# Replacing sixteen TensorE matmuls by accumulating DMAs, and holding weight loads for them, in a gated attention and token-mixing kernel

## The chip, the cores and the metric

The kernel runs on one core of a Trainium2 chip. The metric is the device time of one execution in microseconds (us). The kernel before takes 165.4 us. On one core there are no other cores to compare with, so a run counts as "slow" only when it is over 1.5% above the fastest run of the same kernel; ratios use the fast runs alone.

Engine names in the profile: PE is the matmul engine (TensorE), PEld its weight loads, DVE is VectorE, ACT is ScalarE, POOL is GpSimd, SP is SyncE. POOL and SP mainly issue DMAs here. The granted clock is the share of TensorE's full speed that the profile shows as allowed, 1.00 being all of it.

## The reference, cut to what matters

```python
def reference(A_x, A_wqkv, A_wo, B_x, B_w1, B_b1, B_w2, B_b2, gate_w):   # S=2048, D=512, 32 heads of 16, F=1792
    g = sigmoid((x * gate_w).sum(-1, keepdims=True))                     # x = A_x
    # a: attention over 8 keys, at positions s, s-2, ..., s-14
    qkv = x @ wqkv
    logits = einsum("bhsd,bhswd->bhsw", q, k[gathered]) * 16 ** -0.5     # masked where s-2w < 0
    a = einsum("bhsw,bhswd->bhsd", softmax(logits), v[gathered]) @ wo
    # b: an MLP over the token axis
    u = gelu(einsum("bsd,sf->bdf", layernorm(x), w1) + b1)
    b = transpose(einsum("bdf,fs->bds", u, w2) + b2)
    return g * a + (1 - g) * b
```

## The kernel before

All instructions are handed to a small list scheduler in the kernel, with an estimated duration each. It fixes the order on each engine before the launch; at run time every engine takes its own list in order and waits on semaphores.

The attention logits are products on VectorE: for each of four groups `dl` of four head dimensions, q times shifted k, added into one buffer of 128 partitions by 8 shifts by tokens. Head `i` sits in partitions 4i to 4i+3, so a logit is the sum over four neighbouring partitions. The kernel does the 2048 tokens in two halves, `h` = 0 and 1, each in two parts `s_`. **Before**, TensorE forms that sum for each half with a 0/1 matrix `RP`, and ACT moves the result from PSUM to SBUF:

```python
def f_sum(h, b0, with_gate):                 # 16 matmuls of 512 columns, four at a time in column tiles
    ...                                      # (for h == 0 also the gate's 16 matmuls)
    for wp in range(4):
        for c in range(4):
            ins = e.matmul(ps[32 * c:32 * c + 32, 4 + wp, :], lhsT=RP, rhs=sub(PB[b0], ...), start=True, stop=True, tile_position=(0, 32 * c))
...
A("pe", f_sum(h, b0, h == 0), ..., name="sum%d" % h, prio=-100)
A("act", act(LOG[h], ps[:, 4:8, :], AF.Copy), 1.9, ..., name="lev%d" % h)
A("dve", tt(M4, LOG[h][:, 0:4, :], LOG[h][:, 4:8, :], ALU.max), ..., name="mx4_%d" % h)     # softmax follows
...
# the softmax weights are then spread from 32 to 128 partitions by four DMAs of 512 KB
prev = sch.dma("pool", ..., 524288, name="av%d_%d" % (h, c))
```

The weights multiply the values in eight units `u` of 256 tokens: a product (`avm`, 8192 elements per partition, 4.4 us), then three halving additions `ava`, `avb`, `avc`. For three units the first addition is an accumulating DMA of 1 MB, SBUF to SBUF, on POOL's queue:

```python
AVD = (3, 4, 5)
if u in AVD:
    sch.dma("pool", (lambda o_, i_: lambda e: e.dma_start(o_, i_, accum_op=ALU.add, ...))(pw(0, 4), pw(4, 4)), ..., name="avd%d" % u)
```

The MLP's weights stream in on SP's queue, W1 in seven loads of 1 MB, W2 in eight of 896 KB, each as soon as its buffer is free. The output stores are on the same SP queue:

```python
def ld_w2(j):
    w1ld[7 + j] = load("w2_%d" % j, W2S[j], w2v[:, :, 256 * j:256 * j + 256], F * 256 * 2, ["w2_%d" % j] + W2ALIAS[j], order=False,
                       after=[w1ld[6 + j]])           # 512-byte rows
def finish_tile(i):
    PE(f_wo(i, bank, 0, D), 0.87, ["ot%d" % (i // 2), "wo"], ...)                 # attention's output projection into the same PSUM bank
    A("act", act(OUTS[:, i % 4, :], ps[:, bank, :], AF.Identity, scale=..., bias=...), ...)   # four output buffers
    sch.dma("sp", ... e.dma_start(outv[:, i_, :], OUTS[:, i_ % 4, :]) ..., name="d_out%d" % i)
```

Of the kernel before, what the change touches and what calls it, by code (L numbers as in the profile page):

```python
# [12 lines left out]
S = 2048  # L13
# [56 lines left out]
class _Sched:  # L70
# [73 lines left out]
    def _pass(self, ops, extra, dma_bw, dma_lat):  # L144
# [21 lines left out]
        dma_free = 0.0  # L166
# [8 lines left out]
        while nleft:  # L175
            best = None
            for e in self.ENGS:
                lst = ready[e]
                if not lst:
                    continue  # L180
                bo = None
                bk = None
                for op in lst:
                    st = max(clock[e], rtime[op.idx])
                    if op.table is not None and loaded is not None and op.table != loaded:
                        st += 1.3
                    k = (st, -bl[op.idx] + 3.0 * op.prio, op.idx)
                    if bk is None or k < bk:
                        bk = k
                        bo = op  # L190
                if best is None or bk < best[0]:
                    best = (bk, bo)
            assert best is not None, "scheduler deadlock (cyclic deps?)"
            st = best[0][0]
# [6 lines left out]
            if op.is_dma:  # L201
                clock[e] = st + op.dur
                xs = max(st + 0.3, dma_free)
                xd = max(op.nbytes / dma_bw, 0.05)
                dma_free = xs + xd
                op.end = max(dma_free, clock[e]) + dma_lat
            else:
                op.end = st + op.dur
                clock[e] = op.end
# [98 lines left out]
def bass_gated_mix__sliding_local_dilated__mixer_token_mlp__prompt_kernel(nc, A_x, A_wqkv, A_wo, B_x, B_w1, B_b1, B_w2, B_b2, gate_w, out, dbg=None):  # L308
    with contextlib.ExitStack() as es:
# [11 lines left out]
        for b in range(3):  # L321
# [42 lines left out]
        W1H = [view(n_, BF16, [(256, NST), (1, 256)], extra=k_ * W1N)  # L364
               for n_, k_ in (("W1", 0), ("W1", 1), ("W1", 2), ("XT", 0), ("XT", 1), ("W1", 0), ("W1", 1))]
        W1R = ["w1s0", "w1s1", "w1s2", "w1x0", "w1x1", "w1s0", "w1s1"]

        def w2view(name, extra=0):
            return view(name, BF16, [(256, NFT), (1, 256)], extra=extra)
# [166 lines left out]
        def ld_w1(j):  # L536
            w1ld[j] = load("w1_%d" % j, W1H[j], w1v[:, :, 256 * j:256 * j + 256], S * 256 * 2, [W1R[j]] + (XTALL if j in (3, 4) else []), order=j < 3,
                           after=[w1ld[j - 1]] if j > 3 else [])

        def ld_w2(j):  # L540
            w1ld[7 + j] = load("w2_%d" % j, W2S[j], w2v[:, :, 256 * j:256 * j + 256], F * 256 * 2, ["w2_%d" % j] + W2ALIAS[j], order=False,
                               after=[w1ld[6 + j]])
# [39 lines left out]
        def f_q0(hb, dt):  # L582
            c0, c1 = ((0, 256), (256, 512), (0, 512))[hb]

            def fn(e):
                ins = None
                for dl in range(4):
# [26 lines left out]
        pe_q0(2, 3)  # L614
# [46 lines left out]
        kb0 = [bank_() for dl in range(2)]  # L661
        for k_ in range(2):
            for dl in range(2):
                PE(f_proj(1, dl, 0, kb0[dl], 2 * k_, 2 * k_ + 2), 0.44, XT0 + ["wk%d" % k_], ["b%d" % kb0[dl]], "pjk%d_0_%d" % (dl, k_))
                if k_ == 1:
                    evac(1, dl, 0, kb0[dl])
        for dl in range(2, 4):
# [37 lines left out]
        for t in range(NST):  # L705
            A("dve", (lambda t_: lambda e: e.tensor_scalar(out=X[:, t_, :], in0=X[:, t_, :], scalar1=col(RSTD, t_), scalar2=col(NMR, t_),  # L706
                                                           op0=ALU.mult, op1=ALU.add))(t), 0.33,
              reads=["rstd", "nmr", "st%d" % t], writes=["x%d" % t], name="ln%d" % t, prio=-10)


        def f_sum(h, b0, with_gate):
            def fn(e):
                ins = None
                if with_gate:
                    for dt in range(4):
                        for c in range(4):
                            ins = e.matmul(ps[32 * c:32 * c + 32, 3, :], lhsT=GWREP[:, dt, :],  # L717
                                           rhs=sub(XT, dt * S + c * UT_, [(HS, 2), (1, UT_)]),
                                           start=(dt == 0), stop=(dt == 3), tile_position=(0, 32 * c))
                for wp in range(4):  # L720
                    for c in range(4):
                        ins = e.matmul(ps[32 * c:32 * c + 32, 4 + wp, :], lhsT=RP, rhs=sub(PB[b0], (c // 2) * 4096 + 2 * wp * 512 + (c % 2) * UT_, [(512, 2), (1, UT_)]),  # L722
# [4 lines left out]
        LGB = ["b4", "b5", "b6", "b7"]  # L727
        PLAN = {0: (0, 1, 2), 1: (1, 2, 0)}
        PS = [["p%d_%d" % (b_, s_) for s_ in range(2)] for b_ in range(3)]
        qkd = {}  # L730
        for h in range(2):
            bb = PLAN[h]

            def qk(dl, b_, s_, h=h):
                sb = 2 * h + s_
                A("dve", tt(sub(PB[b_], s_ * 4096, [(512, NW), (1, 512)]), sub(QH[h], dl * HS + s_ * 512, [(0, NW), (1, 512)]),
                            sub(KH[h], dl * KR + PAD + s_ * 512, [(-2, NW), (1, 512)]), ALU.mult), 2.25,
                  reads=["q%d_%d" % (dl, sb), "k%d_%d" % (dl, sb)] + (["k%d_%d" % (dl, sb - 1)] if s_ else ["khalo" if h else "kpad"]),
                  writes=[PS[b_][s_]], name="qk%d_%d_%d" % (h, dl, s_))

            def qadd(x_, y_, s_, h=h):
                A("dve", tt(sub(PB[x_], s_ * 4096, [(1, 4096)]), sub(PB[x_], s_ * 4096, [(1, 4096)]), sub(PB[y_], s_ * 4096, [(1, 4096)]), ALU.add), 2.25,
                  reads=[PS[y_][s_]], writes=[PS[x_][s_]], name="qa%d_%d%d_%d" % (h, x_, y_, s_))
# [12 lines left out]
            for s_ in range(2):  # L756
                qk(3, bb[1], s_)
                qadd(bb[2], bb[1], s_)
            for s_ in range(2):
                qadd(bb[0], bb[2], s_)  # L760
            b0 = bb[0]
            A("pe", f_sum(h, b0, h == 0), 1.2 + (1.0 if h == 0 else 0), reads=PS[b0] + ["rp"] + ((XTALL + ["gwrep"]) if h == 0 else []),
              writes=LGB + (["b3"] if h == 0 else []), name="sum%d" % h, prio=-100, delay=0.2)
            if h == 0:
                A("act", act(E32, ps[:, 3, :], AF.Relu, scale=-1.0, bias=ZMAX), 0.6, reads=["b3"], writes=["e32"], name="zclip")
                A("act", act(EB, E32, AF.Exp, scale=-1.0, bias=ZMAX), 0.6, reads=["e32"], writes=["eb"], name="zexp", table=LOGEXP)
            A("act", act(LOG[h], ps[:, 4:8, :], AF.Copy), 1.9, reads=LGB, writes=["log%d" % h], name="lev%d" % h, prio=-30)
            if h == 0:
                A("dve", tt(psub(LOG[0], 0, 32, 0, [(UT_, NW), (1, PAD)]), psub(LOG[0], 0, 32, 0, [(UT_, NW), (1, PAD)]), MASK, ALU.add), 0.2,
                  reads=["mask"], writes=["log0"], name="msk", prio=-30)  # L770
            TR = ["s4", "s2", "s1"]
            A("dve", tt(M4, LOG[h][:, 0:4, :], LOG[h][:, 4:8, :], ALU.max), 0.65, reads=["log%d" % h], writes=["s4"], name="mx4_%d" % h, prio=-30)
            A("dve", tt(M2, M4[:, 0:2, :], M4[:, 2:4, :], ALU.max), 0.4, reads=["s4"], writes=["s2"], name="mx2_%d" % h, prio=-30)
            A("dve", tt(M1, M2[:, 0, :], M2[:, 1, :], ALU.max), 0.25, reads=["s2"], writes=["s1"], name="mx1_%d" % h, prio=-30)
            A("dve", tt(LOG[h], LOG[h], sub(M1, 0, [(0, NW), (1, UT_)]), ALU.subtract), 1.2, reads=["s1"], writes=["log%d" % h], name="msub%d" % h, prio=-30)
# [7 lines left out]
            A("dve", tt(ATT[h], ATT[h], sub(RB, 0, [(0, NW), (1, UT_)]), ALU.mult), 1.2, reads=["rb"], writes=["att%d" % h], name="nrm%d" % h, prio=-30)  # L783
# [3 lines left out]
            for c in range(4):  # L787
# [4 lines left out]
                al = []  # L792

# [15 lines left out]
        AVD = (3, 4, 5)  # L809
        AVB = (2, 0, 1)  # L810
        avlast = [None]

        def AV(fn, dur, **kw):
            avlast[0] = A("dve", fn, dur, after=[avlast[0]] if avlast[0] else [], **kw)

        def av_parts(u):
            b_ = AVB[u % 3]
# [17 lines left out]
        def av_add(u):  # L835
            res, pv, pw = av_parts(u)
            AV(tt(pw(0, 2), pw(0, 2), pw(2, 2), ALU.add), 1.19, writes=res, name="avb%d" % u)
            AV(tt(OT[:, u], pv[:, 0], pv[:, 1], ALU.add), 0.66, reads=res, writes=["ot%d" % u, OTRES[u]], name="avc%d" % u)

        todo = []  # L840
        for u in range(8):
            av_mult(u)
            if todo and todo[0] + 2 <= u:
                av_add(todo.pop(0))
            if u in AVD:
                todo.append(u)
            else:
                av_add4(u)
                if todo and u == 7:
                    av_add(todo.pop(0))  # L850
                av_add(u)


        def f_ph2(ft, bank, half):
            def fn(e):
                ins = None
                for st in range(8 * half, 8 * half + 8):
                    ins = e.matmul(ps[:, bank, :], lhsT=W1H[ft // 2][:, st, 128 * (ft % 2):128 * (ft % 2) + 128], rhs=X[:, st, :],  # L858
                                   start=(st == 0), stop=(st == NST - 1))
# [3 lines left out]
        MLPB = [1, 2, 0, 1, 2, 0, 3, 1, 2, 0, 3, 1, 2, 0]  # L863
        for ft in range(NFT):
            bank = MLPB[ft]
            for half in range(2):
                PE(f_ph2(ft, bank, half), 1.735, ["x%d" % t for t in range(8 * half, 8 * half + 8)] + [W1R[ft // 2]], ["b%d" % bank],
                   "ph2_%d_%d" % (ft, half))
            A("act", act(UT[:, ft, :], ps[:, bank, :], AF.Gelu_apprx_tanh, bias=col(B1C, ft)), 0.7,
              reads=["b%d" % bank, "b1c"], writes=["ut%d" % ft] + (["wq0", "wq1", "wq2", "wq3", "wk0", "wk1", "wv"] if ft == 0 else []), name="gel%d" % ft, table=GELU)  # L870
            if ft % 2 == 1 and ft // 2 + 5 <= 6:
                ld_w1(ft // 2 + 5)
# [4 lines left out]
        LAG = 5  # L877
        ring[0], ring[1] = 0, [3, 4, 5, 6, 7, 1, 2, 0]
        banks = {}

        def f_ph3(i, bank, half, c0=0, c1=D):
            def fn(e):
                ins = None
                for ft in range(7 * half, 7 * half + 7):
                    ins = e.matmul(ps[:, bank, 0:c1 - c0], lhsT=W2S[i // 2][:, ft, 128 * (i % 2):128 * (i % 2) + 128], rhs=UT[:, ft, c0:c1],  # L885
# [16 lines left out]
        def finish_tile(i):  # L902
            bank = banks[i]
# [5 lines left out]

        L = NST - 1  # L910
        for i in range(L):
            banks[i] = bank_()
        head = ((0, 0), (1, 0), (2, 0), (0, 1), (1, 1), (2, 1))
        for i, half in head + tuple((i, half) for i in range(3, L) for half in range(2)):
            bank = banks[i]
# [103 lines left out]
```

## Time and profile before

| | before |
|---|---|
| time, median (range) | 165.39 us (165.37 to 165.50, 3 runs) |
| span of the profiled run | 163.0 us |
| PE busy | 158.6 us, 97% |
| VectorE busy, and the end of its last unit | 151.1 us, 93%; 157.4 us |
| DMA engine time, loads and stores / POOL's queue | 51.6% / 27.3% of the 16 engines' span |

The summary page of the kernel before: busy time by engine; the DMA queues (q1 is SP's, q0 is POOL's: packets, MB, share of the 16 engines' span); the chain of waits by engine.

```profile
PE 158.6 (97%) x793; PEld 77.2 (47%) x808; DVE 151.1 (93%) x126; ACT 70.2 (43%) x100; POOL 12.0 (7%) x36
...
q1 hardware_dynamic: 41444, 22.06, 51.6%
q0 software_dynamic: 2512, 9.44, 27.3%
...
PE 97%; ACT 1%; issue 1%
```

PE is the bound. It has no gap of a microsecond after the start; the chain is PE almost from end to end.

### The profile page before, as it was taken

The numbers are of one execution on the slowest core, as the hardware profiler recorded it, in microseconds if no ns is written. First come the engines' busy times: TensorE is split into PE (matmuls) and PEld (weight loads), VectorE is DVE, ScalarE is ACT, GpSimd is POOL, SyncE is SP. The second block draws the span as 40 slices with busy tenths as digits, with TensorE's granted clock in tenths as the row PEclk, the third lists the DMA queues.
The fourth block names the chain that finished last, engine by engine and source line by source line (L and its number), as shares of the span: only waits on it lengthen the run. The fifth ranks groups of instructions, "written<-read, shape, count | busy, mean of one in ns | idle before, by whom it ended". The sixth has DMA issues, their size and how long they took to land.

```text
span 163.0 us, 1989 instructions
## 1 busy us (share of the span) xinstructions
PE 158.6 (97%) x793; PEld 77.2 (47%) x808; DVE 151.1 (93%) x126; ACT 70.2 (43%) x100; POOL 12.0 (7%) x36
## 2 busy tenths in 40 slices
PE   7999999999999999999999999999999999999993
PEld 4855555555544344444444344444444444444641
DVE  1789999999999999999999999999999999999961
ACT  3367677666771579662111348011111111111164
POOL 3000030020000000023000000003100222000000
PEclk9999999999999999999999999999999999999999
DMA  5999979729499095999998976981997899991014
GB/s 165 311 268 259 221 183 263 140 38 191 101 277 292 24 242 157 261 290 290 303 245 233 260 188 177 290 209 30 300 243 193 186 207 193 205 216 36 32 59 134
DMA packets 44685, 32.24 MB, mean 198 GB/s; under 512 B 7941, under 2 KB 42245, under 8 KB 44677
## 3 DMA queue, kind: packets, MB, share of 16 engines
q1 hardware_dynamic: 41444, 22.06, 51.6%
q0 software_dynamic: 2512, 9.44, 27.3%
q10 hardware_dynamic: 720, 0.62, 1.2%
q8 instruction: 6, 0.10, 0.2%
q14 instruction: 3, 0.02, 0.0%
HBM read 18.88 MB, written 2.10 MB: 129 GB/s over the span
## 4 chain that ended last, share of the span: by engine, by line
PE 97%; ACT 1%; issue 1%
PE ps L858 30%; PE ps L885 30%; PE ps L649 23%; PE ps L894 8%; PE ps L588 2%; PE ps L551 2%; PE ps L722 1%; ACT arena L453 1%; PE ps L717 1%; PE ps L567 1%; PE ps L604 0%
## 5 line engine op out<-in xcount | busy, mean ns | idle before, releaser
L450 DVE TENSOR_TENSOR arena<-arena 128x4096 bf16<-128x4096 bf16 (+8 forms) x79 | 131.9, 1718 | 1.6 <-ACT arena L453 0.6
L885 PE MATMUL ps<-arena 128*128 128x512 bf16 (+2 forms) x234 | 50.0, 366 | 0.2
L858 PE MATMUL ps<-arena 128*128 128x512 bf16 x218 | 48.5, 379 | 0.3
L453 ACT ACTIVATE arena<-ps,arena 128x512 bf16<-128x512 f32 (+1 forms) x30 | 21.8, 731 | 60.7 <-PE ps L894 37.7
L453 ACT ACTIVATE arena<-ps 128x512 bf16<-128x512 f32 (+3 forms) x53 | 32.9, 629 | 17.4 <-PE ps L649 10.9
L649 PE MATMUL ps<-arena 128*128 128x512 bf16 x173 | 38.0, 379 | 0.2
L885 PEld LDWEIGHTS ps<-arena 128*128 128x128 bf16 x238 | 22.8, 98 | 25.9
L858 PEld LDWEIGHTS ps<-arena 128*128 128x128 bf16 x224 | 21.7, 98 | 26.8 <-issue 0.8
L649 PEld LDWEIGHTS ps<-arena 128*128 128x128 bf16 x176 | 19.9, 113 | 18.0
L894 PE MATMUL ps<-arena 128*128 128x512 bf16 (+2 forms) x67 | 15.6, 366 | 0.1
L453 ACT ACTIVATE arena<-arena 128x16 f32<-128x16 f32 (+5 forms) x10 | 6.7, 678 | 9.7 <-DVE arena L450 9.6
L954 ACT ACT_TABLE_LOAD x7 | 9.0, 1283 | 2.8 <-issue 2.7
L894 PEld LDWEIGHTS ps<-arena 128*128 128x128 bf16 x68 | 6.5, 98 | 7.3
L692 DVE BATCH_NORM_STATS2 arena<-arena 128x6 f32<-128x512 bf16 x16 | 9.9, 679 | 0.1
L790 POOL DMA_DIRECT2D arena<-arena x8 | 4.3, 560 | 75.1 <-DVE arena L450 75.1
L706 DVE TENSOR_SCALAR arena<-arena 128x512 bf16<-128x512 bf16 x16 | 5.3, 404 | 0.0
L827 POOL DMA_DIRECT2D arena<-arena x3 | 3.6, 1209 | 17.7 <-DVE arena L450 17.7
L747 POOL DMA_DIRECT2D arena<-arena x2 | 2.5, 1268 | 30.6 <-DVE arena L692 20.2
L579 DVE CAST arena<-ps 128x256 bf16<-128x256 f32 x4 | 1.6, 422 | 3.2 <-PE ps L567 3.2
L588 PE MATMUL ps<-arena 128*128 128x256 bf16 (+1 forms) x27 | 3.8, 284 | 0.2 <-ACT arena L453 0.2
L551 PE MATMUL ps<-const-bfloat16-1.0 128*128 128x512 bf16 (+1 forms) x9 | 2.7, 483 | 0.8 <-PEq L1004 0.8
L588 PEld LDWEIGHTS ps<-arena 128*128 128x128 bf16 x28 | 2.9, 113 | 0.7 <-DVE arena L579 0.4
(30 smaller groups left out, 14.4 us busy)
## 6 DMA issues: line engine op xcount, KB each, us to landing
arena<-in_B_w_dram SPq DMA_DIRECT2D x7, 1024.0 KB, 6.8
arena<-in_B_w_dram SPq DMA_DIRECT2D x8, 896.0 KB, 9.4
arena<-arena POOLq DMA_DIRECT2D x5, 1024.0 KB, 9.7
arena<-arena POOLq DMA_DIRECT2D x8, 512.0 KB, 11.2
out_dram<-arena SPq DMA_DIRECT2D x15, 128.0 KB, 3.1
arena<-in_A_x_dram SPq DMA_DIRECT2D x3, 512.0 KB, 4.7
arena<-in_A_wqkv_dram SPq DMA_DIRECT2D x2, 256.0 KB, 3.8
arena<-in_A_wqkv_dram SPq DMA_DIRECT2D x1, 512.0 KB, 5.6
```

Source lines behind the costliest of these rows:

```text
L450: return lambda e: e.tensor_tensor(out=o_, in0=a_, in1=b_, op=op_)
L453: return lambda e: e.activation(out=o_, in_=i_, func=f_, **kw)
L551: ins = e.matmul(ps[:, 7, 0:n_], lhsT=C1, rhs=nc.const_aps.tensor(1.0, (128, n_), BF16), start=True, stop=True)
L588: ins = e.matmul(ps[:, dl, c0:c1], lhsT=sub(WQKV, dt * 3 * D + dl, [(4, 128)]), rhs=XT[:, dt, c0:c1], start=(dt == 0 and hb == 0), stop=(d ...
L649: ins = e.matmul(ps[:, bank, :], lhsT=sub(WQKV, dt * 3 * D + tn * D + dl, [(4, 128)]), rhs=XT[:, dt, sb * 512:(sb + 1) * 512], start=(dt = ...
L692: A("dve", (lambda t_: lambda e: e.bn_stats(out=ST6[:, t_, :], in_=X[:, t_, :]))(t), 0.67, reads=["x%d" % t], writes=["st%d" % t], name="s ...
L706: A("dve", (lambda t_: lambda e: e.tensor_scalar(out=X[:, t_, :], in0=X[:, t_, :], scalar1=col(RSTD, t_), scalar2=col(NMR, t_), op0=ALU.mu ...
L790: prev = sch.dma("pool", (lambda d_, s_: lambda e: e.dma_start(d_, s_))(dst, src), 524288, sch.dsem("av%d_%d" % (h, c)), issue=1.0, reads= ...
L858: ins = e.matmul(ps[:, bank, :], lhsT=W1H[ft // 2][:, st, 128 * (ft % 2):128 * (ft % 2) + 128], rhs=X[:, st, :], start=(st == 0), stop=(st ...
L885: ins = e.matmul(ps[:, bank, 0:c1 - c0], lhsT=W2S[i // 2][:, ft, 128 * (i % 2):128 * (i % 2) + 128], rhs=UT[:, ft, c0:c1], start=(ft == 0) ...
L894: ins = e.matmul(ps[:, bank, 0:c1 - c0], lhsT=OT[:, i // 2, dl, 128 * (i % 2):128 * (i % 2) + 128], rhs=WO[:, dl, c0:c1], start=False, sto ...
L954: e.preload_act_table_set(want)
```

## The change

The intent: take the second half's head sums off PE, the bounding engine (16 matmuls and one ACT eviction), and give them to DMAs that add in flight; keep the DMA engines clear for them by holding some W2 loads; and take work off VectorE. The parts:

1. Second half's head sums by 12 DMAs on POOL's queue: four add partition 4i+2 onto 4i and 4i+3 onto 4i+1 (256 KB each), four copy partition 4i into the logits (128 KB each), four add partition 4i+1 to them (128 KB each). I call them folds. The products are laid out anew for them.
2. W2 load 2 waits for the first-stage folds, W2 load 3 for the last fold, W2 load 6 for the last of the second half's weight broadcasts. I call these the holds.
3. The accumulating additions go to units 2, 4, 5; a new order of the units.
4. Block 0's last Q matmuls signal per `dl`, and K of block 0 is no longer started on the first half of its weights; the gate's matmuls move earlier; eight of sixteen normalizations move to ACT.
5. W1 and W2 loads have 1 KB rows; the two MLP matmuls are regrouped by four tiles and half contractions. The scheduler's own DMA model is changed too.

```diff
+            if h:
+                fas = {}
+                for s_ in range(2):
+                    for k_ in range(2):
+                        fas[s_] = fold("fa%d_%d%d" % (h, s_, k_), par(PB[b0], k_, [(4 * pst, 32), (1, 4096)], s_ * 4096), par(PB[b0], k_ + 2, ...),
+                             True, 550000, [PS[b0][s_]], ["fa%d_%d%d" % (h, s_, k_)])
+                for s_ in range(2):
+                    for k_ in range(2):
+                        for c in (2 * s_, 2 * s_ + 1):
+                            fl = fold("%s%d_%d" % ("fb" if k_ == 0 else "fc", h, c), psub(LOG[h], 32 * c, 32, 0, [(1, NW * UT_)]), par(PB[b0], k_, ...),
+                                 k_ == 1, 100000 * (1 + k_), [PS[b0][s_], "fa%d_%d%d" % (h, s_, k_)], ["log%d_%d" % (h, c)], ...)
+                folds += [fas[1], fl]
+            else:
+                A("pe", f_sum(b0), 1.0, ...)
+                A("act", act(LOG[h], ps[:, 4:8, :], AF.Copy), 1.9, ...)
...
         def ld_w2(j):
-            w1ld[7 + j] = load("w2_%d" % j, W2S[j], w2v[:, :, 256 * j:256 * j + 256], F * 256 * 2, ["w2_%d" % j] + W2ALIAS[j], order=False,
+            w1ld[7 + j] = load("w2_%d" % j, W2S[j], w2v[:, 7 * (j % 2):7 * (j % 2) + 7, 512 * (j // 2):512 * (j // 2) + 512], F * 256 * 2, ["w2_%d" % j] + W2ALIAS[j], order=False, deps={2: folds[0:1], 3: folds[1:2], 6: avc_last}.get(j, []),
                                after=[w1ld[6 + j]])
...
-        AVD = (3, 4, 5)
+        AVD = (2, 4, 5)
...
-        kb0 = [bank_() for dl in range(2)]
-        for k_ in range(2):
-            for dl in range(2):
-                PE(f_proj(1, dl, 0, kb0[dl], 2 * k_, 2 * k_ + 2), 0.44, XT0 + ["wk%d" % k_], ["b%d" % kb0[dl]], ...)
...
+        for dl in range(4):
             proj(1, dl, 0)
...
+            if t >= NST - 8:
+                A("act", act(X[:, t, :], X[:, t, :], AF.Identity, scale=col(RSTD, t), bias=col(NMR, t)), 0.6, ..., name="ln%d" % t, prio=8)
+                continue
```

## The prediction

It was written from the kernel before, its trace and the diff alone.

> **What bounds the kernel now.** TensorE. The summary shows PE busy 97% of the 163.0 us span (158.6 us) at granted clock 1.0; the chain of waits is PE for 97%, from 0.85 to 159.5 us, then two ACT evictions (1.34 us) and the last store. In the chain, 14 matmuls of 512 columns take 3.02 us, 0.2157 us each. The Trainium skill, "TensorE: Matmul & The Clock Gate", section "Wait — 56ns, not 53.3ns?", gives 215.7 ns as the warm spacing at 512 columns; this trace agrees, so matmuls here can only be removed, not hurried. VectorE is the close second: 93% busy, back to back until 157.4 us (timeline), about 1 us before the last output projections need its last tile.
>
> **What the change does.**
> 1. Second half's head sums leave PE: 16 column-tiled matmuls, 0.86 us of the chain at 91.9 us. This is the only PE work removed. The 1.88 us ACT eviction goes too. The gate's 0.98 us of matmuls only moves earlier.
> 2. In their place come 12 DMAs on the POOL queue. Estimate: existing accumulating DMAs issue in 1.2 us and land about 9.7 us after issue for 1 MB; the folds move a quarter or less each, in three dependent rounds, so the logits are ready 10 to 13 us after the last second-half product instead of about 3. VectorE has the first half's value products meanwhile (8.5 us for a whole unit), so most is hidden; I expect 0 to 3 us of VectorE waiting before the maximum, or before the fourth unit (held behind the weights).
> 3. Eight of 16 normalizations move from VectorE (0.33 us each in sequence, 2.6 us) to ACT, 43% busy, with gaps of 0.27 us between evictions and banks as buffer. Splitting Q's first signal starts VectorE about 0.5 us sooner. Together about 3 us for VectorE, which pays for step 2; it should finish near 154 to 157 us.
> 4. Weight loads: same bytes, 1 KB rows for 512 B. Loads now land in 6.8 to 9.4 us and nothing on PE waited for them. The holds delay W2 parts 2, 3 and 6 until folds and broadcasts are through; each has estimated slack of over 4 us. Zero on the chain.
> 5. MLP reordering by groups of four gives ACT more room. PE did not wait for gelu before, so zero.
> 6. Accumulating adds on units 2, 4, 5 instead of 3, 4, 5: same number, same VectorE time.
>
> **Sum.** On the critical path: -0.86 us, perhaps +0.1 to +0.5 of small new waits. 165.39 - 0.86 gives 164.5. **Predicted 164.5 us, range 163.9 to 166.0**; faster by over 2% 0.02, within 2% 0.93, slower by over 2% 0.05.
>
> **What would show it.** Right: chain still PE about 97%, the second group of head-sum matmuls gone, matmul spacing unchanged, PE ending near 158.7 us; VectorE busy falls about 3 us, with a wait of a few us near 100 to 125 us; POOL issues rise by 12; ACT gains eight normalizations of about 0.65 us. Wrong on step 2: output projections wait for VectorE. Wrong on 4: PE in the second MLP matmul waits for a weight DMA. Wrong on 3: PE waits for ACT around 36 to 50 us.
>
> **What would make it wrong.** Folds taking over 20 us because POOL issues queue up or collide with weight loads: then the last value tiles pass PE's end and each us costs one. Or the ACT normalizations arriving late, idling PE at the start of the MLP. A gain above 2% would need PE work to vanish that I don't see.

## More of the kernel before

The late stretch, in a table of windows (us from the start; busy time of each engine with instruction counts, granted PE clock, share of DMA engine time, GB/s), has PE full in every window. (A DMA packet's whole time is counted where it starts, so a share can pass 1.)

```profile
88.00:100.00 12.00, 11.89 (x67) 5.18 (x67) 11.86 (x8) 4.96 (x5) 0.00 (x0) 1.00 0.72 198
100.00:112.00 12.00, 11.95 (x56) 5.44 (x56) 11.90 (x10) 2.94 (x4) 0.00 (x0) 1.00 0.87 219
...
136.00:148.00 12.00, 11.95 (x56) 5.49 (x56) 11.86 (x8) 2.33 (x3) 0.15 (x1) 1.00 0.92 187
148.00:160.00 12.00, 11.95 (x72) 6.27 (x71) 9.30 (x6) 5.12 (x7) 0.00 (x0) 1.00 0.16 55
```

The column to remember is the last but one: the DMA engines are 72 to 92% busy in three of the four windows. They are no bound, since nothing on PE waits for them, but there is little room. The first two windows hold W2 loads, the third holds two of the accumulating DMAs. SP's queue over time shows that all W2 loads go out in the first stretch, the last at 112.4 us, before the first store:

```profile
65.03 47.77 SPq L494 DMA_DIRECT2D arena<-in_B_w_dram  x10
118.01 42.67 SPq L907 DMA_DIRECT2D out_dram<-arena  x15
```

## The result

| | before | after |
|---|---|---|
| time, median (range) | 165.44 us (165.37 to 165.65, 4 runs) | 172.44 us (171.02 to 174.28, 4 runs) |
| ratio of the fast runs, 95% interval | | 1.0373 (1.0307 to 1.0439) |

The change makes the kernel 3.7% slower. The prediction said 164.5 us, at most 166.0, and gave "slower by over 2%" a chance of 0.05. It was wrong. (All ratios here are the recorded ones, formed from the means of the fast runs of the same rounds, so not quite the ratio of the medians. Two runs of the changed kernel here, 174.28 and 173.60 us, are slow; the ratio rests on 171.02, 171.29 and 172.64 us.)

The profile taken with this result fell on a slow run. I ran the unchanged "after" kernel again, below, and read its fast profile here. It is that of the fastest of four runs (171.46 us). The slow profile has one PE wait more, 2.1 us for W2 load 3 near 116 us, and VectorE ends at 161.0 us in it; I do not explain what only that run shows. Its summary page:

```profile
PE 160.1 (94%) x777; PEld 77.1 (46%) x792; DVE 149.0 (88%) x118; ACT 70.0 (41%) x105; POOL 21.5 (13%) x48
...
PE   7999999999999999999999999999999993978993
...
PEclk9999999999999999999999999999999999699999
...
q1 hardware_dynamic: 28132, 22.06, 45.4%
q0 software_dynamic: 3216, 11.54, 36.0%
...
PE 76%; DMA 15%; SPq 5%; ACT 1%; issue 1%; ACTq 0%
```

The 16 matmuls are gone (777 for 793). PE has holes in slices 34 and 36 of 40, and the granted clock dips in slice 35. DMAs are now in the chain. POOL's queue takes 36.0% of 169.4 us where it took 27.3% of 163.0 us: 61.0 against 44.5 us of the whole set of 16 engines, so 16.5 us of DMA engine time more, for 2.1 MB more moved. Not all of that is the folds: `e5_pe_sums_no_hold` below, which has none, takes 48.9 us on this queue (29.7% of 164.7 us), and `e7_before_folds`, the kernel before with the folds, 56.1 us (30.2% of 185.7 us). So the folds take 11.7 to 12.1 us, by these two differences.

Where PE waits: the view of waits of the same run (who waited for what: total us, times, longest).

```profile
ACT arena L455 <- DMA out_dram<-arena: 12.5, 1, 12.5
...
PE ps L926 <- DMA arena<-in_B_w_dram: 2.9, 1, 2.9
...
PE ps L926 <- ACT arena L455: 1.6, 1, 1.6
```

L926 is the second MLP matmul, which had no such waits before. The timeline of PE at that place (start, length, what, count, idle time before and its releaser):

```profile
140.23 1.03 PE L935 MATMUL ps<-arena 128*128 128x512 bf16 x4
144.12 4.87 PE L926 MATMUL ps<-arena 128*128 128x512 bf16 x14 [2.86 <-DMA arena<-in_B_w_dram]
149.04 0.81 PE L935 MATMUL ps<-arena 128*128 128x512 bf16 x3
149.69 1.67 PE L926 MATMUL ps<-arena 128*128 128x512 bf16 x7
153.01 1.31 PE L926 MATMUL ps<-arena 128*128 128x384 bf16 x7 [1.65 <-ACT arena L455]
```

The first wait is for W2 load 6. The second is for a PSUM bank that ACT can't empty, because its output buffer still belongs to a store in flight. SP's queue tells why both are late:

```profile
119.44 8.21 SPq L948 DMA_DIRECT2D out_dram<-arena  x3
133.56 1.99 SPq L496 DMA_DIRECT2D arena<-in_B_w_dram  x2
135.59 6.44 SPq L948 DMA_DIRECT2D out_dram<-arena  x4
```

W2 loads 6 and 7 went out at 133.56 us. That is the moment at which the last of the four broadcasts landed, by the trace's completion times: the hold ends there. In the kernel before, load 6 went out at 99.5 us. The fourth store stood in SP's list behind the two loads, and went out at 135.59 us. The DMA view, for issues between 130 and 142 us of the same run (size, median us to landing), shows what the loads met then:

```profile
arena<-arena POOLq DMA_DIRECT2D x2, 1024.0 KB, 11.7
arena<-in_B_w_dram SPq DMA_DIRECT2D x2, 896.0 KB, 14.1
out_dram<-arena SPq DMA_DIRECT2D x4, 128.0 KB, 12.9
```

They ran against the accumulating DMAs of units 4 and 5. Load 6 took 10.4 us and load 7 took 17.8 us. The fourth store landed 16.5 us after its issue. A store with nothing beside it takes 1.7 us (the last stores of both kernels). The windows show PE's loss and the clock:

```profile
136.00:148.00 12.00, 9.14 (x36) 3.63 (x35) 11.20 (x8) 1.55 (x2) 1.22 (x1) 0.87 1.02 228
148.00:160.00 12.00, 10.30 (x54) 4.92 (x54) 9.58 (x6) 2.22 (x3) 0.00 (x0) 0.99 0.49 144
```

The clock record has one dip to 0.5 in this stretch, from 144.92 us for 3.41 us. The Trainium skill, "TensorE: Matmul & The Clock Gate", section "What's actually happening", says that the clock is halved after an idle window of about 3.4 us. The trace agrees with the half clock and the length of 3.41 us; it shows the dip after an idle time of only 2.86 us.

The sum for this run, from matmul start times. PE's last matmul ends at 166.83 us, before at 160.38 us: 6.45 us later. Gap for load 6: 3.02 us over the normal spacing. Gap for the bank: 1.81 us. The half clock: 3.41 / 2 = 1.71 us. A later first K projection: 9.36 against 8.59 us, 0.77 us, of which 0.43 us is a wait for the second half of the K weights. Less the matmuls removed, 0.86 us. That is 6.45 us. (In the result above the fast runs' means differ by 6.2 us; slower runs of the changed kernel have more, which this trace does not show.)

VectorE, which I had feared for, ends its last unit at 157.68 us in this run, as before (157.41 us). So far this says which waits came last. Whether the holds, the folds, or the rest of the change caused them is for the experiments.

### The profile page after: what moved, and what is told of

The parts are those of the page before. It is cut to its first block, busy times and chain, and to the rows that moved or that the text cites. A ratio compares the mean times of both kernels' runs of the same rounds, so it can differ in the third digit from the quotient of the medians.

```text
span 172.3 us, 1969 instructions
## 1 busy us (share of the span) xinstructions
PE 160.0 (93%) x777; PEld 76.9 (45%) x792; DVE 149.1 (87%) x118; ACT 69.7 (40%) x105; POOL 21.5 (12%) x48
## 4 chain that ended last, share of the span: by engine, by line
DMA 39%; DVE 26%; PE 18%; SPq 7%; issue 5%; ACT 1%; POOL 1%; ACTq 0%; POOLq 0%
DVE arena L452 23%; DMA arena<-arena 19%; PE ps L926 13%; DMA out_dram<-arena 10%; SPq L495 6%; DMA arena<-in_B_w_dram 6%; PE ps L935 5%; DMA arena<-in_A_x_dram 4%; DVE arena L708 2%; DVE arena L690 1%; SPq L496 1%; ACT arena L455 1%; POOL arena L787 1%; DVE arena L680 0%; DVE arena L701 0%
## 5 line engine op out<-in xcount | busy, mean ns | idle before, releaser
L452 DVE TENSOR_TENSOR arena<-arena 128x4096 bf16<-128x4096 bf16 (+7 forms) x79 | 132.7, 1720 | 5.8 <-DMA arena<-arena 3.9
L926 PE MATMUL ps<-arena 128*128 128x512 bf16 (+2 forms) x236 | 52.1, 375 | 6.9 <-DMA arena<-in_B_w_dram 5.2
L926 PEld LDWEIGHTS ps<-arena 128*128 128x128 bf16 x238 | 23.0, 100 | 34.8 <-issue 5.8
L455 ACT ACTIVATE arena<-ps 128x512 bf16<-128x512 f32 (+3 forms) x52 | 30.4, 604 | 12.1 <-PE ps L653 6.6
L894 PEld LDWEIGHTS ps<-arena 128*128 128x128 bf16 x224 | 21.8, 98 | 26.6 <-issue 0.4
L653 PEld LDWEIGHTS ps<-arena 128*128 128x128 bf16 x176 | 19.7, 113 | 18.3 <-ACT arena L455 0.4
L455 ACT ACTIVATE arena<-arena 128x512 bf16<-128x512 bf16 (+6 forms) x18 | 13.3, 739 | 22.3 <-DVE arena L452 21.0
L935 PE MATMUL ps<-arena 128*128 128x512 bf16 (+2 forms) x64 | 15.1, 366 | 0.2
L787 POOL DMA_DIRECT2D arena<-arena x12 | 9.5, 947 | 24.6 <-DMA arena<-arena 23.1
L828 POOL DMA_DIRECT2D arena<-arena x8 | 4.7, 605 | 49.7 <-DVE arena L452 49.7
L935 PEld LDWEIGHTS ps<-arena 128*128 128x128 bf16 x68 | 6.5, 98 | 7.2
L759 POOL DMA_DIRECT2D arena<-arena x2 | 2.5, 1267 | 28.6 <-DVE arena L690 21.6
L867 POOL DMA_DIRECT2D arena<-arena x3 | 3.9, 1299 | 15.8 <-DVE arena L452 15.8
```

The source lines that it names most:

```text
L452: return lambda e: e.tensor_tensor(out=o_, in0=a_, in1=b_, op=op_)
L455: return lambda e: e.activation(out=o_, in_=i_, func=f_, **kw)
L653: ins = e.matmul(ps[:, bank, :], lhsT=sub(WQKV, dt * 3 * D + tn * D + dl, [(4, 128)]), rhs=XT[:, dt, sb * 512:(sb + 1) * 512], start=(dt = ...
L787: return sch.dma("pool", lambda e: e.dma_start(o_, i_, **kw), nb, sch.dsem(name), issue=1.1, reads=reads, writes=writes, name=name, after= ...
L828: prev = sch.dma("pool", (lambda d_, s_: lambda e: e.dma_start(d_, s_))(dst, src), 524288, sch.dsem("av%d_%d" % (h, c)), issue=1.0, reads= ...
L894: ins = e.matmul(ps[:, bank, :], lhsT=w_, rhs=X[:, st, :], start=(st == 0), stop=(st == NST - 1))
```

## The experiments

Theory A: the holds make W2 loads 3 and 6 late, and the stores behind them (load 3's wait was seen in the slow profile). Theory B, its first rival: the folds cost the time themselves, since VectorE gets the logits late. After the first four runs I formed theory C: the folds take DMA engine time in the stretch that W2 used, so that either the logits or the weights come late, and the holds only choose which. Its rival D: it is the new unit order, the regrouped MLP or the normalization on ACT. Every run gave a correct result.

### The same kernel again, and the holds taken apart

`e0_after_again` is the changed kernel without an edit. The three others change only the explicit waits of W2 loads; the orders of all engines other than SP are the same.

```diff
 # e1_no_holds
-    deps={2: folds[0:1], 3: folds[1:2], 6: avc_last}.get(j, []),
 # e2_hold_folds
-    deps={2: folds[0:1], 3: folds[1:2], 6: avc_last}.get(j, []),
+    deps={2: folds[0:1], 3: folds[1:2]}.get(j, []),
 # e3_hold_w26
-    deps={2: folds[0:1], 3: folds[1:2], 6: avc_last}.get(j, []),
+    deps={6: avc_last}.get(j, []),
```

> The changed kernel unmodified, for a second trace on the chip the variants use. Both theories expect 171 to 174 us with the same three PE gaps (about 2.3 us near 116, 3.3 us near 143, 1.8 us near 154, in us from the span's start).

> All three explicit W2 holds removed, every other engine's order unchanged. Theory A (the holds make W2 parts 3 and 6 late, and the store queue waits behind part 6): all three gaps in the second MLP matmul go; VectorE then ends at 161 us or so and is what is left, so 167 to 169 us. Rival B (the folds themselves, through VectorE being late, cost the time): 171 us or more, since folds and loads now also collide. If neither VectorE nor loads matter: 164.5 to 166.

> Only the hold of W2 part 6 on the broadcasts removed; parts 2 and 3 still wait for the folds. Theory A: the gaps near 143 and 154 us go together (the latter is a bank that waits for a store queued behind part 6), the one near 116 us stays; 167.5 to 170 us. Rival B: 171 us or more.

> Only the holds of W2 parts 2 and 3 on the folds removed; part 6 still waits for the broadcasts. Theory A: the gap near 116 us (2.3 us) goes, the other two stay; 168.5 to 172 us. Rival B: 171 us or more, gap near 116 us unchanged.

Measured, with the kernel before at 165.50 us in the same rounds:

| run | holds | median us (range) | ratio (95% interval) |
|---|---|---|---|
| `e0_after_again` | 2, 3 and 6 | 173.41 (171.46 to 176.68) | 1.0394 (1.0340 to 1.0448) |
| `e1_no_holds` | none | 174.36 (173.52 to 175.76) | 1.0515 (1.0463 to 1.0566) |
| `e2_hold_folds` | 2 and 3 | 170.71 (169.90 to 173.71) | 1.0295 (1.0251 to 1.0340) |
| `e3_hold_w26` | 6 | 177.52 (176.25 to 178.96) | 1.0697 (1.0636 to 1.0758) |

Slow by the rule, and not in the ratios, are two runs of `e0_after_again` (174.12 and 176.68 us) and one each of `e2_hold_folds` and `e3_hold_w26`. With them in, the means are 173.7, 174.5, 171.3 and 177.6 us in the order of the table: that all holds beat none is then within the spread, while the effects read below keep their direction.

Not all went as expected. `e0_after_again` shows two of the three gaps that I had taken from the slow profile; the one near 116 us is not there, and is 0.3 us in `e2_hold_folds`. `e3_hold_w26` is far outside theory A's 168.5 to 172 us. My expectation of 167 to 169 us without holds missed by 5 us. Theory A is half right. The hold of load 6 costs: 1.0295 to 1.0394 with the other holds, 1.0515 to 1.0697 without them. The holds of loads 2 and 3 help: from 1.0515 to 1.0295. They protect something. The waits of `e1_no_holds` show what:

```profile
DVE arena L452 <- DMA arena<-arena: 11.2, 2, 9.5
...
PE ps L935 <- DVE arena L452: 8.8, 3, 6.0
```

Without holds PE no longer waits for W2 at all. VectorE waits 9.5 us in one piece for the logits, all later units slide, and PE waits 8.8 us for their output (L935 is the output projection). The DMA view for issues between 86 and 102 us shows the competition. With holds 2 and 3 (`e0_after_again`) one W2 load is issued there and the 128 KB folds land in 4.0 us at the median:

```profile
arena<-arena POOLq DMA_DIRECT2D x8, 128.0 KB, 4.0
arena<-in_B_w_dram SPq DMA_DIRECT2D x1, 896.0 KB, 5.5
```

Without holds (`e1_no_holds`) it is four W2 loads:

```profile
arena<-in_B_w_dram SPq DMA_DIRECT2D x4, 896.0 KB, 17.8
arena<-arena POOLq DMA_DIRECT2D x6, 128.0 KB, 7.1
```

The last fold landed 17.8 us after the last product of the second half (87.84 to 105.66 us) with the holds, and 26.6 us after it (88.11 to 114.75 us) without. The loads suffer as well: 17.8 us at the median. In `e0_after_again` the first two W2 loads, issued at 70.5 and 77.4 us beside the first folds and the first half's broadcasts, took 21.7 and 21.6 us to land.

`e2_hold_folds` removed both gaps behind load 6, as expected, and got 1.6 us for it by the fast means, 2.7 us by the medians. At 170.71 us it lies between what theory A (at most 170 us) and rival B (at least 171 us) had named: another wait took the place. VectorE waited 4.6 us for the accumulating DMA of unit 4, which landed 13.0 us after issue, and PE waited 3.4 us for that unit's output.

### The folds given back to PE; stores on another queue; the folds alone in the kernel before

```diff
 # e4_pe_sums: PE sums for both halves, first MLP matmul on banks 0 to 3 (4 to 7 receive the sums); holds 2 and 3 vanish with the folds
-            if h:
+            if False:
                 fas = {}
...
-            bank = (0, 1, 2, 3, 0, 1, 4, 5, 6, 7, 2, 3, 0, 1)[ft]
+            bank = (0, 1, 2, 3, 0, 1, 2, 3, 0, 1, 2, 3, 0, 1)[ft]
 # e5_pe_sums_no_hold: the same, and hold 6 removed
 # e6_stores_act: the changed kernel with its stores on ACT's queue
-            sch.dma("sp", ... e.dma_start(outv[:, i_, :], OUTS[:, i_ % 4, :]) ...
+            sch.dma("act", ... e.dma_start(outv[:, i_, :], OUTS[:, i_ % 4, :]) ...
 # e7_before_folds: the kernel BEFORE, with the 12 folds in place of sum1 and lev1, and the product layout that they need
+            if h:
+                for s_ in range(2):
+                    for k_ in range(2):
+                        fold("fa%d_%d%d" % (h, s_, k_), ...)
...
+            else: A("pe", f_sum(h, b0, h == 0), ...
```

> The changed kernel with the second half's head sums given back to TensorE (16 matmuls and the ACT eviction), the first MLP matmul on banks 0 to 3 only; with no folds the holds of W2 parts 2 and 3 fall away, the hold of part 6 on the broadcasts stays; everything else of the change stays. Theory C (the fold DMAs take DMA engine time and latency in the stretch from 72 to 106 us that W2 used before, so either the logits or the weights come late): 164.8 to 166.5 us, weights broadcast issued near 110 us instead of 117 to 120, no PE gap above 1 us. Rival D (the new order of the value units, the regrouped MLP or ACT normalization costs the time): stays above 169 us.

> As the run before, and the hold of W2 part 6 taken away too. Theory C: 164.8 to 166 us, within 0.5 us of the run with the hold (without folds the hold is harmless). If the hold costs by itself: at least 1 us faster than the run with it. Rival D: above 169 us.

> The changed kernel, with the 15 output stores issued from ACT's queue instead of SP's, where W2 parts 6 and 7 wait and load ahead of them. If the gap near 151 to 154 us (1.8 us) is a bank held by a store queued behind part 6, it goes, and the time falls by about 2 us to 169 to 170.5; the gap near 141 us (part 6 landing late) stays. If that gap has another cause, it stays and the time is 171 to 173.

> The kernel before with one part of the change alone: the second half's head sums by the same 12 DMAs (with the product layout they need), no holds, weights in 512-byte rows as before. Theory C: slower than before, 168 to 174 us, logits ready 17 to 30 us after the last second-half product and VectorE waiting several us for them; PE then waits for VectorE in the output projections. Rival D (the folds are innocent): 164.5 to 166 us.

Measured, with the kernel before at 165.89 us in the same rounds:

| run | median us (range) | ratio (95% interval) |
|---|---|---|
| `e4_pe_sums` | 173.85 (173.26 to 175.35) | 1.0472 (1.0422 to 1.0522) |
| `e5_pe_sums_no_hold` | 166.47 (165.82 to 166.88) | 1.0035 (0.9995 to 1.0075) |
| `e6_stores_act` | 174.27 (171.97 to 175.32) | 1.0463 (1.0381 to 1.0545) |
| `e7_before_folds` | 189.08 (187.71 to 189.41) | 1.1386 (1.1331 to 1.1442) |

**Rival D falls.** With neither folds nor holds, and everything else of the change kept, the time is that of the kernel before within the interval. PE has no gap over half a microsecond in it after the start; its page, with the busy share of PE in 40 slices and POOL's queue:

```profile
PE 160.0 (97%) x793; PEld 77.6 (47%) x808; DVE 148.9 (90%) x118; ACT 77.0 (47%) x110; POOL 12.1 (7%) x36
...
PE   7999999999999999999999999999999999999993
...
q0 software_dynamic: 2512, 9.44, 29.7%
```

(The scheduler orders the other engines anew where the folds are gone, so the runs without folds differ from the changed kernel in order too; the two of them share one order on all engines but SP.)

**The folds and hold 6 are two causes, and each is enough.** The folds without holds: 1.0515 (`e1_no_holds`, other rounds) against 1.0035 without them. Hold 6 without folds: 1.0472 against 1.0035, 7.4 us by the medians; the edit between these two is the hold alone. I had expected the hold to be harmless without folds, and that was wrong. In `e4_pe_sums` SP's queue is the same picture as above, though the logits are early:

```profile
99.83 0.97 SPq L496 DMA_DIRECT2D arena<-in_B_w_dram  x2
121.15 3.10 SPq L948 DMA_DIRECT2D out_dram<-arena  x2
133.85 2.08 SPq L496 DMA_DIRECT2D arena<-in_B_w_dram  x2
135.97 2.66 SPq L948 DMA_DIRECT2D out_dram<-arena  x1
```

The broadcasts were issued from 112.66 us, 1.1 us after the accumulating DMA of unit 2 on the same queue; the last landed at 133.84 us, 19.6 us after its issue, and load 6 went out 0.01 us later. Here it is the third store that waits behind it, and PE then waits for the bank:

```profile
ACT arena L455 <- DMA out_dram<-arena: 13.8, 1, 13.8
...
PE ps L926 <- ACT arena L455: 5.4, 1, 5.4
```

And the stretch in which load 6 could have run stood half empty. Windows of `e4_pe_sums`; before, the DMA shares of these two were 0.72 and 0.87:

```profile
88.00:100.00 12.00, 11.84 (x67) 5.23 (x67) 11.79 (x12) 7.16 (x6) 0.00 (x0) 1.00 0.37 125
100.00:112.00 12.00, 11.95 (x57) 5.42 (x56) 11.93 (x8) 6.52 (x8) 0.47 (x1) 1.00 0.47 153
```

**The folds alone, in the kernel before, are far worse**, 1.1386; I had expected 168 to 174 us. Nothing is held, the weights have short rows, and VectorE waits 22.2 us for DMAs, 11.2 us of it in one piece for the logits; PE waits 18.1 us in one piece for VectorE, and the PE clock is then at half for 17.07 us. So the rest of the change softens the folds. I did not take apart which part does.

**Stores on ACT's queue** removed the gap near 151 us, as that theory said: PE no longer waits for a bank. But the time did not fall by 2 us, against what I wrote. PE's waits for W2 grew: 1.0 us near 116 us, and for load 6 5.2 us in one piece, where it was 2.9 us, since load 6 went out at 136.05 us and landed 11.4 us later, at 147.46 us. The Trainium skill, "DMA: Bandwidth & Descriptors", section "Issuing engines are not separate DMA queues", says that DMAs run on the same 16 engines whichever engine starts them, and that another queue only saves time on the sequencer. These runs agree: in `e6_stores_act` the fourth store, on its own queue, went out at 129.21 us and landed 7.6 us later, not the 1.7 us of a lone store, beside the broadcasts. What the other queue gained it was the earlier issue, 129.21 us for 135.59 us: it no longer stood behind the held loads.

### The start of K; the folds by themselves; the best version with folds

```diff
 # e8_pe_sums_old_k: e5_pe_sums_no_hold, with K of block 0 as in the kernel before
+        kb0 = [bank_() for dl in range(2)]
...      (the seven lines that the change removed)
 # e9_hold_all_w2: the changed kernel, holds replaced by one
-    deps={2: folds[0:1], 3: folds[1:2], 6: avc_last}.get(j, []),
+    deps={0: folds[1:2]}.get(j, []),
 # e10_folds_unit4_dve: e2_hold_folds, with K of block 0 as before, and
-        AVD = (2, 4, 5)
+        AVD = (2, 5)
-        AVORDER = "... m4 m5 m6 b4 c4 a6 b6 c6 m7 b5 c5 a7 b7 c7"
+        AVORDER = "... m4 a4 b4 c4 m5 m6 a6 b6 c6 m7 b5 c5 a7 b7 c7"
 # e11_hold_all_folds: e9 mended, the first W2 load waits for all eight second-stage folds
+    deps=folds[1:] if j == 0 else [],
...
+                            fcs.append(fl)
-                folds += [fas[1], fl]
+                folds += [fas[1]] + fcs
```

> The run without folds and holds, and K of block 0 for the first two heads' groups started again on the first half of the K weights, as in the kernel before. That run and the changed kernel waited 0.45 us for the second half of the K weights near 9 us. If that wait is all that separates the run without folds from the kernel before: 0.3 to 0.6 us faster than it, so the same as before within 0.5 us (ratio 0.997 to 1.003). If something else of the change still costs: ratio of 1.003 or more.

> A measurement, not a proposal: all W2 loads wait until the last fold has landed, so the folds meet no W2 load. Logits came 17.8 us after the last second-half product with two parts held and 26.8 us with none. If the excess is competition for the DMA engines: 10 to 16 us here. If it is the chain's own latency: 17 us or more still. TensorE then waits for W2 from about 97 us on, so the whole is slow, 175 to 190 us.

> The best version with folds that I can form: no hold on W2 part 6, K of block 0 started as before, and the first addition of unit 4 done by VectorE instead of an accumulating DMA that landed 13 us after its issue and made VectorE wait 4.6 us and TensorE 3.6 us. If those waits are what was left: the gap near 145 us goes, VectorE ends near 160 us, 166 to 168.5 us. It doesn't beat the kernel before unless VectorE ends before 157 us. If competition moves the wait elsewhere: 169 us or more.

> The measurement of the run before again, mended: there the scheduler finished the other half first, so the W2 loads were released when only that half's folds had landed. Here the first W2 load waits for all eight second-stage folds. In that run, folds of 128 KB landed 2.7 to 4.7 us after issue before the loads started and 7.8 to 8.2 us after. If competition with the loads is what stretches the chain: the last fold lands 12 to 16 us after the last second-half product, every second-stage fold in under 5.5 us. If it is the chain's own latency: 17 us or more. TensorE waits about 10 us for W2 near 98 us; 174 to 182 us.

| run | median us (range) | before, same rounds | ratio (95% interval) |
|---|---|---|---|
| `e8_pe_sums_old_k` | 166.04 (165.09 to 167.05) | 165.55 | 1.0038 (0.9998 to 1.0078) |
| `e9_hold_all_w2` | 171.74 (one run) | 165.55 | none |
| `e10_folds_unit4_dve` | 167.32 (166.00 to 168.86) | 165.55 | 1.0082 (1.0042 to 1.0122) |
| `e11_hold_all_folds` | 175.84 (one run) | 165.43 | none |

`e8_pe_sums_old_k`: the wait of 0.45 us for K weights near 9 us is gone from the trace, but the ratio did not move (1.0038 against 1.0035). What is left is at the edge of what these rounds resolve; whether 0.4% remains, and from what, stays open.

`e9_hold_all_w2` did not do what I wanted. The new wait changed the scheduler's priorities, the other half of the products finished first, and the loads were released at 95.5 us with three folds under way and two still to be issued. That split is telling in itself: folds of 128 KB issued before the loads landed 2.7 to 5.2 us after issue, the two issued after them 7.8 and 8.2 us.

`e11_hold_all_folds` settles it. All W2 loads wait for the folds. The DMA view, issues between 86 and 102 us:

```profile
arena<-in_B_w_dram SPq DMA_DIRECT2D x2, 896.0 KB, 5.8
arena<-arena POOLq DMA_DIRECT2D x8, 128.0 KB, 4.1
arena<-arena POOLq DMA_DIRECT2D x2, 256.0 KB, 4.9
```

The last fold lands 13.5 us after the last product (87.50 to 101.02 us), each second-stage fold in 3.3 to 4.6 us, and VectorE does not wait for the logits. The chain's own latency is 13.5 us; what is over that, at 17.8 us with two loads held and 26.6 us with none, is competition with the W2 loads. It is paid on the other side: PE waits 7.3 us for W2 at 98 us, and the whole takes 175.8 us.

`e10_folds_unit4_dve` is the best version with folds that I found. Its summary page:

```profile
PE 159.9 (97%) x792; PEld 77.0 (47%) x792; DVE 151.3 (92%) x119; ACT 72.2 (44%) x107; POOL 20.2 (12%) x47
...
q1 hardware_dynamic: 28132, 22.06, 46.4%
q0 software_dynamic: 2944, 10.49, 32.6%
```

The gap near 145 us is gone. It still is 0.8% slower than the kernel before: PE waits 0.6 us for W2 load 3, and 0.8 us in two pieces for VectorE, whose last unit ends at 160.47 us. VectorE is now as busy as in the kernel before, for a gain of 0.86 us on PE that it can't use. No version beat the kernel before.

The set as a whole, by ratio to before:

| | no holds | holds 2, 3 | hold 6 | all |
|---|---|---|---|---|
| folds | 1.0515 | 1.0295 | 1.0697 | 1.0394 |
| PE sums | 1.0035 | (need folds) | 1.0472 | |

## Why the prediction was wrong

- **What bounds the kernel, and what the change takes away: right.** PE bounds it, matmul spacing did not change (0.2157 us at full clock), and the 16 matmuls are gone. The gain of 0.86 us is in the sum of the result.
- **Step 4 failed, and it is the step that counts.** I wrote that the holds delay "W2 parts 2, 3 and 6 until folds and broadcasts are through; each has estimated slack of over 4 us. Zero on the chain." The slack rested on landing times of 6.8 to 9.4 us, which are the medians of the W1 and W2 loads; beside the first half's broadcasts a W2 load took up to 16.1 us in the kernel before, whose own last broadcast of the second half landed 13.9 us after its issue, at 128.20 us. Both could have been read before the change. Load 6 was released at 133.6 us, because a broadcast took up to 14.7 us to land (19.6 us in `e4_pe_sums`), and then took 10.4 us itself against two accumulating DMAs. It was 3 us late. Hold 6 costs 7.4 us without any folds.
- **I missed that SP's list is in order.** A held load stops the stores behind it, and a late store holds an output buffer, a PSUM bank, and then PE: 1.8 us in the changed kernel, 5.4 us in `e4_pe_sums`. `e6_stores_act` shows that this link is real: on another queue that gap goes.
- **Step 2 was nearly right alone and wrong in company.** "The logits are ready 10 to 13 us after the last second-half product": 13.5 us when no W2 load runs beside them (`e11_hold_all_folds`), 17.8 us in the changed kernel, 26.6 us without holds. VectorE waited 0.6 us for them in the changed kernel, inside the 0 to 3 us that I gave; without the holds it is 9.5 us. My list of what could make it wrong named this collision, folds taking over 20 us, but I gave it too small a chance. I costed latency on POOL's queue and not the 12 us or so of DMA engine time that the folds take, in a stretch that was 72 to 87% full with W2.
- **The clock was left out.** A PE gap of 2.9 us set the clock to half for 3.41 us and added 1.7 us. I treated waits as adding one for one.
- **Step 3: right in direction.** VectorE's busy time fell by 2.1 us (151.1 to 149.0 us), not 3. An ACT normalization took 0.80 us, not 0.65, and PE did not wait for it. The gain went into waiting, and in the fast profile VectorE ended when it had ended before.
- **Step 5: right** (`e5_pe_sums_no_hold` shows no gap). I did not see that K of block 0 now waits for both halves of its weights: 0.43 us of PE time in that trace.
- **Step 6: right for VectorE's busy time only.** Waiting for the accumulating DMA of unit 4 cost 3.4 us on PE once hold 6 was gone (`e2_hold_folds`).
- **1 KB rows**: the share of SP's queue fell from 51.6% of 163.0 us to 46.4% of 164.7 us (`e5_pe_sums_no_hold`), 84.1 to 76.4 us of DMA engine time for the same bytes. That is real, off the critical path as predicted, and less than the 12 us or so that the folds take.

## What to carry to other kernels

Moving work from a bounding engine to DMAs is free only if the DMA engines have idle time in that same stretch: add the engine time of the new DMAs to the window's DMA share first, and read landing times from a stretch as loaded as the new one will be. A hold on a load is a bet on when the awaited DMA lands; it also holds everything behind that load in the same list, here the output stores, so place it only where the release is early by more than a loaded transfer takes. And a wait of a few microseconds on PE costs more than its length, since the clock may drop after it.

## What the Trainium skill lacked or had wrong

- "TensorE: Matmul & The Clock Gate", section "What's actually happening", has the clock halve after an idle window of about 3.4 us. In `e0_after_again` PE was idle for 2.86 us and the clock was halved for 3.41 us from 144.9 us; in `e1_no_holds` gaps with starts 1.66 and 1.97 us apart did not do it, nor did 2.35 us of idle time in `e7_before_folds`. So less than 3.4 us of idle time was enough here; no run was made to find the least, or whether it depends on where the gap falls.
- "DMA: Bandwidth & Descriptors", section "Anatomy of one DMA — SWDGE (gpsimd) path", gives about 2.0 us plus bytes over 436e3 for one DMA, which makes an estimate of 2.3 us for 128 KB. Folds of 128 KB (32 partitions, copy or accumulate) took 3.3 to 4.6 us with no W2 load beside them and 6.2 to 8.1 us beside three or four. The page has no figure for an accumulating DMA: 1 MB, SBUF to SBUF, landed 7.8 to 14.4 us after issue in the kernel before and in `e0_after_again`, and up to 19.4 us in `e7_before_folds`.
- The same page, section "Specifications", calls 512 B the least transfer for line rate. Rows of 1 KB for 512 B still cut the engine time of SP's queue from 84.1 to 76.4 us at the same bytes.
- No page that I read puts a number on what a held load costs the stores behind it in the issuing engine's list: in `e0_after_again` the fourth store left at 135.59 us, behind two held loads (129.21 us on a queue of its own in `e6_stores_act`), and then took 16.5 us to land where a store alone takes 1.7 us.
